# Attention of a gated mixer: a fixed plan for TensorE's side work, six rotating score banks, six value visits per group

## The chip, the cores and the metric

The kernel runs on one core of a Trainium2 chip. The metric is the device time of one execution in microseconds (us), the median of several runs. An execution has one more time, the span: from the first to the last instruction that the profiler recorded. TensorE is called PE below and its weight loads PEld; VectorE is DVE, ScalarE is ACT, GpSimd is POOL, and SyncE, which issues most of the DMAs, is SP.

## The reference

Two branches read the same input `x` (2048 tokens, 448 features) and are mixed token by token by a gate. Branch A is attention with 16 heads of 28 features that share one set of keys and values:

```
q = (x @ wq) split into 16 heads;  k = x @ wk;  v = x @ wv
scores = einsum("bhqd,bkd->bhqk", q, k) * 28 ** -0.5
a = (softmax(scores) @ v) merged @ wo
```

Branch B is a spatial-shift MLP: layer norm, `w1`, gelu, a shift of four channel quarters by one or two tokens, `w2`, a residual; then layer norm, `w3` (to 1792), gelu, `w4`, a residual. The result is `g * a + (1 - g) * b` with `g = sigmoid(x . gate_w)`. All data are 32-bit floats.

## The kernel before

The kernel works through branch B first (about 20 us to 424 us of the span) and through attention after it. The keys, the values and the first two groups of queries are made at the beginning.

Attention is cut into 16 groups, `u = 0..15`. A group is one block of 512 queries (`b = u // 4`) with four of the sixteen heads (`g = u % 4`). Within a group the 2048 keys are 16 key tiles `kt` of 128. A running number `k = 16 u + kt` counts key tiles over all groups.

For one key tile PE makes four score matmuls (line 663, one for each head `j`, 128 keys by 512 queries), each into a PSUM bank of its own. ACT turns each into `p = exp(s)` (line 665) and so frees the bank. The value products (`pv_group`, line 625) multiply the tile's `p` with the values of that key tile: four matmuls for each tile, one for each head in a 32-column strip of the array, each of which the profile shows as two instructions. They add up over the 16 tiles in one bank (`mx`), whose row of sums gives the softmax's denominator. They come in visits: after every second key tile (`PVB = 2`) PE makes the products of two tiles, which lie `LAG = 2` tiles behind the scores. A group so has eight visits.

PE has more work in attention, and all of it is written between the scores by hand:

- `q_job(u + 2)`, 11 matmuls (line 503): the queries of the group after the next. At its end `q_evac` (lines 144 to 151) reads the result's bank with ACT (`qh`, line 147) and then with DVE (`ql`, line 148), and three DMAs of SP spread it.
- `max_part(u + 1, t)`, four times four small matmuls (line 166), each four followed by a DVE maximum that reads the bank (line 167); then `max_rows`, one matmul (line 193) whose bank ACT copies (`mrow`, line 195), with two DMAs.
- `norm_job`, one matmul (line 543) that spreads the reciprocal sums of the group before; DVE multiplies from that bank (line 545), POOL splits the result into two parts (lines 548 and 549).
- `wo_job(b, t)`, 12 matmuls for 128 tokens of the output projection (lines 556 to 560), four of them for each block of queries once its four groups are done, each with a DVE operation that mixes in branch B (line 564) and a DMA out.

`q_job`, `norm_job` and `wo_job` are generators kept in a list `jobs`; `pump()` is called after every second score matmul and takes one step (about one matmul) of the job at hand. Jobs enter the list when a key tile's number is reached (`kt == 2` for queries, `k + 6` and `k + 8` after a group's end for the others). `max_part`, `max_end` and `max_rows` aren't pumped: they stand after the tiles `kt` = 6 to 11.

The order of PE's instructions is the order in which the program writes them (`manual_schedule(engines={PE})`). The order on the other engines and all waits are made by the framework's scheduler. A PSUM tile of a tag with `bufs = n` takes one of n banks in turn; the first instruction that writes it waits until all readers of that bank's former tile are done.

PSUM's eight banks in attention are: `mm` two, `misc` one and `s` two for scores (the tile `n % 5` picks among five); `m` two for all the other work (`m_tile`, also under the name `misc_tile`); `mx` one for the value products. That makes eight. In the last group `s_tile` uses three score banks only, as the two banks of `s` hold parts of the last output projection.

## Time and profile before

| | |
|---|---|
| median of 3 runs | 1071.31 us (1070.52 to 1072.3) |
| the profiled execution | 1070.98 us, of which the span is 1069.1 us |
| PE busy, matmuls | 1039.7 us (97%) |
| PE busy, weight loads | 679.6 us (64%) |
| ACT busy | 673.2 us (63%) |
| DVE busy | 258.0 us (24%) |
| POOL busy | 159.8 us (15%) |
| attention, first to last score matmul | 423.9 us to 1049.5 us |

PE's busy time is modelled, since matmuls overlap in its pipeline; a busy PE need not be at its peak. The chain of waits is followed back from the last instruction and names for each stretch the work that held up the end; its pieces are given with their start, their length and their count. In the timeline a row stands for some merged instructions of one line (start, length, engine, line, operation, result and inputs, count) and, in brackets, the idle time of the engine ahead of it with what ended it. A view by windows gives for each stretch of time the busy time of each engine, with the clock that was granted to PE (1.00 is full) as the third number from the end.

### The profile page before, as it was taken

To read this page: it belongs to the slowest core of one execution; us is meant where nothing else is said; L and a number is where in the kernel's file an instruction comes from. 1 tells how busy PE (TensorE), PEld (TensorE's weight loads), DVE (VectorE), ACT (ScalarE), POOL (GpSimd) and SP (SyncE) were. 2 spreads that over 40 slices of the span, in tenths; PEclk is the share of its full clock that TensorE was granted. 3 is DMA by queue.
4 is the path that set the end of the run, shared out by engine and by line. 5 is a ranking of instruction groups with operands and counts; after the bars stand their busy time and mean duration, and the time that the engine had idled before them with its cause. 6 is when DMAs were issued, how large, how long until landed. Compare 5 with 4: busy or idle time off the path is not lost.

```text
span 1069.1 us, 13948 instructions
## 1 busy us (share of the span) xinstructions
PE 1039.7 (97%) x5610; PEld 679.6 (64%) x5610; DVE 258.0 (24%) x521; ACT 673.2 (63%) x1318; POOL 159.8 (15%) x182
## 2 busy tenths in 40 slices
PE   6999889999999999999999999999999999999995
PEld 4787778888888888454554555554655555555542
DVE  6744952311411311401110110120110210111102
ACT  5444451222222223788888888889888889888873
POOL 5622430110200201603000002010002100000100
PEclk9999899999999999999999999999999999999998
DMA  9401330000000000423211202220202220211001
GB/s 312 131 1 37 111 111 1 1 1 1 1 1 1 1 1 29 164 32 70 33 17 16 31 20 40 39 31 3 39 10 41 39 31 2 40 24 26 10 2 38
DMA packets 30541, 41.15 MB, mean 38 GB/s; under 512 B 8004, under 2 KB 20100, under 8 KB 30340
## 3 DMA queue, kind: packets, MB, share of 16 engines
q1 hardware_dynamic: 30324, 40.04, 16.3%
q8 instruction: 46, 0.75, 0.3%
q14 instruction: 27, 0.22, 0.1%
q10 hardware_dynamic: 144, 0.13, 0.1%
HBM read 23.28 MB, written 3.67 MB: 25 GB/s over the span
## 4 chain that ended last, share of the span: by engine, by line
PE 91%; DVE 4%; DMA 1%; ACT 1%; POOL 1%; issue 1%; SPq 0%; POOLq 0%; ACTq 0%; DVEq 0%
PE s L663 27%; PE pv L625 22%; PE acc L420 4%; PE acc L419 4%; PE acc L421 4%; PE g L115 4%; PE g L116 4%; PE g L117 4%; PE q L503 3%; PE m L166 2%; PE wo L560 1%; PE wo L558 1%; PE wo L556 1%; PE g L119 1%; PE g L118 1%; PE h L116 1%
## 5 line engine op out<-in xcount | busy, mean ns | idle before, releaser
L665 ACT ACTIVATE p<-s 128x512 f32<-128x512 f32 x1024 | 517.6, 627 | 98.1 <-PE s L663 97.8
L663 PE MATMUL s<-qs,kS 98*128 98x512 f32 x1024 | 343.6, 420 | 1.4 <-ACT p L665 0.7
L663 PEld LDWEIGHTS s<-qs,kS 98*128 98x128 f32 x1024 | 181.6, 189 | 168.2 <-ACT p L665 127.1
L625 PE MATMUL pv<-p,vext 128*32 128x512 f32 x2048 | 247.6, 602 | 0.0
L409 ACT ACTIVATE gh<-g 128x512 fp32r<-128x512 f32 x56 | 33.6, 600 | 174.9 <-PE g L119 174.9
L625 PEld LDWEIGHTS pv<-p,vext 128*32 128x32 f32 x2048 | 53.7, 109 | 107.6 <-issue 100.3
L411 DVE TENSOR_TENSOR gl<-gf,gh 128x512 fp32r<-128x512 f32 x56 | 41.3, 738 | 192.1 <-ACT gf L410 192.0
L419 PE MATMUL acc<-w4h,gh 128*128 128x448 f32 x224 | 82.6, 369 | 0.0
L420 PE MATMUL acc<-w4l,gh 128*128 128x448 f32 x224 | 82.0, 366 | 0.0
L421 PE MATMUL acc<-w4h,gl 128*128 128x448 f32 x224 | 81.7, 365 | 0.0
L167 DVE TENSOR_REDUCE mr<-m 128x4 f32<-128x512 f32 x64 | 44.3, 692 | 146.0 <-PE m L166 145.3
L548 POOL CAST onh<-on 128x512 fp32r<-128x512 f32 x15 | 9.2, 614 | 414.8 <-DVE on L545 228.7
L115 PE MATMUL g<-ah,w3h 128*128 128x512 f32 x168 | 67.1, 399 | 3.1 <-ACT gf L410 2.8
L116 PE MATMUL g<-al,w3h 128*128 128x512 f32 x168 | 66.5, 396 | 0.1
L117 PE MATMUL g<-ah,w3l 128*128 128x512 f32 x168 | 66.3, 394 | 0.0
L521 DVE SCALAR_TENSOR_TENSOR good<-rt,good 128x16 f32<-128x16 f32 x15 | 2.6, 175 | 190.2 <-DMA rt<-o 190.2
L419 PEld LDWEIGHTS acc<-w4h,gh 128*128 128x128 f32 x224 | 42.0, 188 | 4.9
L420 PEld LDWEIGHTS acc<-w4l,gh 128*128 128x128 f32 x224 | 42.1, 188 | 4.8
L421 PEld LDWEIGHTS acc<-w4h,gl 128*128 128x128 f32 x224 | 42.0, 188 | 3.6
L166 PEld LDWEIGHTS m<-kS,qs 96*128 96x128 f32 x256 | 38.4, 191 | 6.3 <-DVE mr L167 1.2
L115 PEld LDWEIGHTS g<-ah,w3h 128*128 128x128 f32 x168 | 31.9, 190 | 9.7 <-ACT gf L410 3.3
L564 DVE SCALAR_TENSOR_TENSOR ot<-wo,gg,x 128x448 f32<-128x448 f32 x16 | 10.9, 682 | 108.0 <-PE wo L560 108.0
(204 smaller groups left out, 1144.4 us busy)
## 6 DMA issues: line engine op xcount, KB each, us to landing
qs<-qh SPq DMA_DIRECT2D x32, 256.0 KB
qs<-ql SPq DMA_DIRECT2D x16, 256.0 KB
xq<-in_xT_dram SPq DMA_DIRECT2D x4, 1024.0 KB
x<-in_x_dram SPq DMA_DIRECT2D x4, 896.0 KB
w3raw<-in_w_dram SPq DMA_DIRECT2D x7, 512.0 KB
out_dram<-ot SPq DMA_DIRECT2D x16, 224.0 KB
w4raw<-in_w_dram SPq DMA_DIRECT2D x7, 448.0 KB
xkv<-in_xT_dram SPq DMA_DIRECT2D x3, 1024.0 KB
```

Of the source, the lines that this page charges most:

```text
L115: nc.tensor.matmul(ps, wh[:, c, :], ah[:, c, :], start=(c == 0), stop=False)
L116: nc.tensor.matmul(ps, wh[:, c, :], al[:, c, :], start=False, stop=False)
L117: nc.tensor.matmul(ps, wl[:, c, :], ah[:, c, :], start=False, stop=False)
L166: nc.tensor.matmul(ps[:, j, :], q_of[u][0:96, j, t * P:(t + 1) * P], kS[0:96, 0:MK], start=True, stop=True)
L167: nc.vector.reduce_max(mx_of[u][:, :, t], ps, axis=AX.X)
L411: nc.vector.tensor_sub(gl, gf, f32(gh))
L419: nc.tensor.matmul(ps, gh[:, tok], w4h[i][:, k, :], start=(f == 0), stop=False)
L420: nc.tensor.matmul(ps, gh[:, tok], w4l[i][:, k, :], start=False, stop=False)
L421: nc.tensor.matmul(ps, gl[:, tok], w4h[i][:, k, :], start=False, stop=(f == NF - 1))
L625: nc.tensor.matmul(pv[32 * j:32 * j + 32, :], vext[:, kt, :], ps[j], start=(kt == 0), stop=(kt == NT - 1), tile_position=(0, 32 * j))
L663: nc.tensor.matmul(ps, kS[0:98, kt * P:(kt + 1) * P], q_of[u][0:98, j, :], start=True, stop=True)
L665: nc.scalar.activation(p, ps, AF.Exp, scale=SCALE)
```

## The change

A group's side work now follows a plan. Each key tile has two slots, after its second and after its fourth score matmul, so a group has slots 0 to 31. `units(u)` lists (first slot, generator) pairs; at each slot PE gets one step of the generator at hand, and where that one ends, of the next whose first slot has come. For most groups the list is: `q_job(u + 2)` from slot 0, the maxima of the next group from slot 12 (one `max_part` a slot), the normalisation from 16, `max_rows` from 17, and one `wo_job` of the former block from 18 (so the output projection of a block is spread over the four groups of the next). In group 0 the maxima start at slot 4, `max_rows` at 12 and `q_job(2)` at 20. The last matmul of a generator is now followed by a `yield` of its own: what reads its bank (`q_evac`, the DVE product of `norm_job`, `gate_out`) is written one slot later, behind that slot's two scores.

The banks are dealt out again: six for scores (`mm` two, `misc`, and three single ones, `s0` to `s2`), four of them in the last group; one (`m`) for all the other work; `mx` as before.

The value products come in six visits per group, after the scores of the key tiles 3, 6, 9, 12, 14 and of tile 0 of the next group. They take all tiles up to the one before the tile just scored: three, three, three, three, two and two tiles.

The input tile `raw` has one buffer in place of two, so the loads of `wq`, of the first `x` block and of `wo` come one after the other; the first block's low part is made by DVE in place of POOL. `onh` and `onl` have seven buffers in place of five. In the last group only four of the twelve (`t`, `g`) parts of the last output projection with `g < 2` run between scores; the others stand in the rewritten tail, between its transposes.

```diff
-LAG = 2
-PVB = 2
+VISITS = (3, 6, 9, 12, 14, 16)
...
         def m_tile(name):
-            return ps3.tile([P, 512], F32, tag="m", bufs=2, name=name)
...
+            return ps3.tile([P, 512], F32, tag="m", bufs=1, name=name)
...
+        def s_more(i):
+            return lambda name: ps3.tile([P, 512], F32, tag=f"s{i}", bufs=1, name=name)
+
+        s_tiles = (mm_tile, mm_tile, s_spare, s_more(0), s_more(1), s_more(2))
+
         def s_tile(n, last=False):
-            return (mm_tile, mm_tile, s_spare, s_more, s_more)[n % (3 if last else 5)](f"s_{n}")
+            return s_tiles[n % (4 if last else 6)](f"s_{n}")
...
-            raw = s3.tile([P, 4, 512], F32, tag="raw", bufs=2, name=f"xq_{b}")
+            raw = s3.tile([P, 4, 512], F32, tag="raw", bufs=1, name=f"xq_{b}")
...
-            (nc.gpsimd if b else nc.vector).tensor_copy(ah, raw)
-            nc.gpsimd.tensor_tensor(al, raw[:, 0:3, :], f32(ah)[:, 0:3, :], ALU.subtract)
+            eng = nc.gpsimd if b else nc.vector
+            eng.tensor_copy(ah, raw)
+            eng.tensor_tensor(al, raw[:, 0:3, :], f32(ah)[:, 0:3, :], ALU.subtract)
...
             for n, (w, a) in enumerate(ops):
                 nc.tensor.matmul(ps, w, a, start=(n == 0), stop=(n == 10))
-                if n < 10:
-                    yield
+                yield
...
             q_evac(s3, u, ps, q_of[u])
-            yield
...
             nc.tensor.matmul(ps, sel8, rb, start=True, stop=True)
+            yield
             on = s3.tile([P, 512], F32, tag="onf", bufs=2, name=f"on_{u}")
...
+        def max_units(u):
+            for t in range(4):
+                max_part(u, t, m_tile)
+                if t == 3:
+                    max_end(u)
+                yield
+
+        def row_unit(u):
+            max_rows(u, m_tile)
+            yield
...
+        def units(u):
+            b, g = divmod(u, NG)
+            wo = [(18, wo_job(b - 1, g))] if b else []
+            norm = [(16, norm_unit(u - 1))] if u else []
+            if u == 0:
+                return [(4, max_units(1)), (12, row_unit(1)), (20, q_job(2))]
+            if u < NU - 2:
+                return [(0, q_job(u + 2)), (12, max_units(u + 1))] + norm + [(17, row_unit(u + 1))] + wo
+            if u < NU - 1:
+                return [(12, max_units(u + 1))] + norm + [(17, row_unit(u + 1))] + wo
+            return [(0, wo_early(t, g)) for t in range(2) for g in range(2)] + norm + wo
...
-        def pv_group(k):
...
+        def visit(u, k0, k1):
...
+            for kt in range(k0, k1):
+                ps = p_of.pop((u, kt))
+                for j in range(4):
+                    nc.tensor.matmul(pv[32 * j:32 * j + 32, :], vext[:, kt, :], ps[j],
+                                     start=(kt == 0), stop=(kt == NT - 1), tile_position=(0, 32 * j))
+            if k1 == NT and u < NU - 1:
+                norm_of[u] = recip_begin(u, pv_of.pop(u))
...
                     p_of[u, kt].append(p)
+                    if j % 2 == 1:
+                        while True:
+                            if job is None:
+                                if not plan or plan[0][0] > 2 * kt + j // 2:
+                                    break
+                                job = plan.pop(0)[1]
+                            try:
+                                next(job)
+                                break
+                            except StopIteration:
+                                job = None
...
+            if kt in VISITS or kt == 0 and u:
+                v = VISITS.index(kt or NT)
+                visit(u if kt else u - 1, VISITS[v - 1] if v else 0, VISITS[v])
...
+        tail_wo(0, 2)
+        tail_wo(1, 2)
+        tail_a(0)
+        tail_a(1)
+        tail_wo(2, 0)
+        tail_wo(2, 1)
...
+        tail_wo(3, 1)
+        tail_wo(3, 2)
+        tail_wo(2, 3)
+        tail_wo(3, 3)
```

More of the change, by code (lines that the diff above doesn't have):

```diff
@@ L466, in m_tile @@
         def m_tile(name):
-            return ps3.tile([P, 512], F32, tag="m", bufs=2, name=name)
-        def s_more(name):
-            return ps3.tile([P, 512], F32, tag="s", bufs=2, name=name)
+            return ps3.tile([P, 512], F32, tag="m", bufs=1, name=name)
         def misc_tile(name):
@@ L543, in norm_job @@
             nc.tensor.matmul(ps, sel8, rb, start=True, stop=True)
+            yield
             on = s3.tile([P, 512], F32, tag="onf", bufs=2, name=f"on_{u}")
             nc.vector.tensor_mul(on, o, ps)
-            onh = s3.tile([P, 512], F32R, tag="onh", bufs=5, name=f"onh_{u}")
-            onl = s3.tile([P, 512], F32R, tag="onl", bufs=5, name=f"onl_{u}")
+            onh = s3.tile([P, 512], F32R, tag="onh", bufs=7, name=f"onh_{u}")
+            onl = s3.tile([P, 512], F32R, tag="onl", bufs=7, name=f"onl_{u}")
             nc.gpsimd.tensor_copy(onh, on)
@@ L550, in norm_job @@
             on_of[u] = (onh, onl)
-            yield
         def wo_group(ps, b, t, g, first, last):
@@ L570, in wo_job @@
                 yield from wo_group(ps, b, t, g, g == 0, g == NG - 1)
-                if g < NG - 1:
-                    yield
             gate_out(4 * b + t, ps)
-            yield
-        wqraw = s3.tile([P, 4, 512], F32, tag="raw", bufs=2, name="wqraw")
+        wqraw = s3.tile([P, 4, 512], F32, tag="raw", bufs=1, name="wqraw")
         nc.sync.dma_start(wqraw, wq)
@@ L587, in gated_mix_kernel @@
         split_wq(2, 4)
+        split_wq(0, 2)
         load_x(0)
-        woraw = s3.tile([P, 4, 512], F32, tag="raw", bufs=2, name="woraw")[:, :, 0:D]
+        woraw = s3.tile([P, 4, 512], F32, tag="raw", bufs=1, name="woraw")[:, :, 0:D]
         nc.sync.dma_start(woraw, wo.rearrange("(g p) n -> p g n", p=P))
-        split_wq(0, 2)
         nc.gpsimd.tensor_copy(woh, woraw)
@@ L596, in gated_mix_kernel @@
             nc.gpsimd.tensor_scalar(x1[:, n, :], x1[:, n, :], gi[:, n:n + 1], None, op0=ALU.mult)
-        jobs = []
-        current = [None]
-        def pump():
-            if current[0] is None:
-                if jobs:
-                    current[0] = jobs.pop(0)()
-                    next(current[0])
-            else:
-                try:
-                    next(current[0])
-                except StopIteration:
-                    current[0] = None
-        def drain():
-            while current[0] is not None or jobs:
-                pump()
+        norm_of = {}
@@ new lines, in gated_mix_kernel, with norm_unit, wo_early @@
+        wo_last = []
+        def max_units(u):
[6 more added lines that the diff above has]
+            max_rows(u, m_tile)
+            yield
+        def norm_unit(u):
+            yield from norm_job(u, *norm_of.pop(u))
+        def wo_early(t, g):
+            if g == 0:
+                wo_last.append(s_tiles[5 - t](f"wo_{NB - 1}_{t}")[:, 0:D])
+            yield from wo_group(wo_last[t], NB - 1, t, g, g == 0, False)
@@ new lines, in rest @@
+        def rest():
+            yield
+        def units(u):
[9 more added lines that the diff above has]
+            return [(0, wo_early(t, g)) for t in range(2) for g in range(2)] + norm + wo
@@ L616, in gated_mix_kernel @@
         p_of, pv_of = {}, {}
-        def pv_group(k):
-            u, kt = divmod(k, NT)
-            if kt == 0:
+        def visit(u, k0, k1):
+            if k0 == 0:
                 pv_of[u] = max_tile(f"pv_{u}")
             pv = pv_of[u]
-            ps = p_of.pop(k)
-            for j in range(4):
-                nc.tensor.matmul(pv[32 * j:32 * j + 32, :], vext[:, kt, :], ps[j],
-                                 start=(kt == 0), stop=(kt == NT - 1), tile_position=(0, 32 * j))
-            if kt == NT - 1 and u < NU - 1:
-                o, rb = recip_begin(u, pv_of.pop(u))
-                delayed.append((k + 6, lambda: norm_job(u, o, rb)))
-                if u == NU - 2:
-                    for t in range(4):
-                        delayed.append((k + 10, lambda t=t: wo_last_job(t, NG - 2)))
-                elif u % NG == NG - 1:
-                    for t in range(4):
-                        delayed.append((k + 8, lambda t=t: wo_job(u // NG, t)))
@@ L637, in gated_mix_kernel @@
-        wo_last = []
-        def wo_last_job(t, g):
-            if g == 0:
-                wo_last.append((m_tile if t < 2 else s_more)(f"wo_{NB - 1}_{t}")[:, 0:D])
-            yield from wo_group(wo_last[t], NB - 1, t, g, g == 0, False)
-            yield
-        delayed = []
-        for k in range(NU * NT + LAG):
-            u, kt = divmod(k, NT)
-            while delayed and delayed[0][0] <= k:
-                jobs.append(delayed.pop(0)[1])
-            if k == (NU - 1) * NT:
-                for g in range(NG - 2):
-                    for t in range(4):
-                        jobs.append(lambda t=t, g=g: wo_last_job(t, g))
+            for kt in range(k0, k1):
[3 more added lines that the diff above has]
+                                     start=(kt == 0), stop=(kt == NT - 1), tile_position=(0, 32 * j))
@@ L654, in gated_mix_kernel @@
+            if k1 == NT and u < NU - 1:
+                norm_of[u] = recip_begin(u, pv_of.pop(u))
+        for k in range(NU * NT + 1):
+            u, kt = divmod(k, NT)
             if k < NU * NT:
-                if kt == (7 if u == 0 else 2) and u + 2 < NU:
-                    jobs.insert(0, lambda u=u: q_job(u + 2))
+                if kt == 0:
+                    plan = units(u)
+                    at, job = 0, None
                 if kt == 8 and (u + 3) % NG == 0 and u + 3 < NU:
                     load_x((u + 3) // NG)
-                p_of[k] = []
+                p_of[u, kt] = []
@@ L663, in gated_mix_kernel @@
                     nc.tensor.matmul(ps, kS[0:98, kt * P:(kt + 1) * P], q_of[u][0:98, j, :], start=True, stop=True)
-                    p = s3.tile([P, 512], F32, tag="p", bufs=4 * (LAG + PVB) + 2, name=f"p_{n}")
+                    p = s3.tile([P, 512], F32, tag="p", bufs=18, name=f"p_{n}")
                     nc.scalar.activation(p, ps, AF.Exp, scale=SCALE)
-                    p_of[k].append(p)
-                    if j % 2 == 1 or u == NU - 1:
-                        pump()
-                if u + 1 < NU:
-                    if 6 <= kt < 10:
-                        max_part(u + 1, kt - 6, m_tile)
-                    elif kt == 10:
-                        max_end(u + 1)
-                    elif kt == 11:
-                        max_rows(u + 1, m_tile)
-            if k >= LAG and k % PVB == PVB - 1:
-                for kk in range(k - LAG - PVB + 1, k - LAG + 1):
-                    if kk >= 0:
-                        pv_group(kk)
-        assert not delayed
-        drain()
+                    p_of[u, kt].append(p)
+                    if j % 2 == 1:
[9 more added lines that the diff above has]
+                                job = None
+                if kt == NT - 1:
+                    if job is not None:
+                        for _ in job:
+                            pass
+                    for _, job in plan:
+                        for _ in job:
+                            pass
+            if kt in VISITS or kt == 0 and u:
+                v = VISITS.index(kt or NT)
+                visit(u if kt else u - 1, VISITS[v - 1] if v else 0, VISITS[v])
         u = NU - 1
@@ L685, in gated_mix_kernel @@
         o = s3.tile([P, 512], F32, tag="o", bufs=2, name=f"o_{u}")
-        onh = s3.tile([P, 512], F32R, tag="onh", bufs=5, name=f"onh_{u}")
-        onl = s3.tile([P, 512], F32R, tag="onl", bufs=5, name=f"onl_{u}")
+        onh = s3.tile([P, 512], F32R, tag="onh", bufs=7, name=f"onh_{u}")
+        onl = s3.tile([P, 512], F32R, tag="onl", bufs=7, name=f"onl_{u}")
         on_of[u] = (onh, onl)
@@ L706, in tail_b, with tail_wo @@
             nc.vector.tensor_sub(onl[:, toks[t]], tq, f32(onh)[:, toks[t]])
-        def tail_c(t):
-            for _ in wo_group(wo_last[t], NB - 1, t, NG - 1, False, True):
-                pass
-            gate_out(4 * (NB - 1) + t, wo_last[t])
+        wo_last.append(m_tile(f"wo_{NB - 1}_2")[:, 0:D])
+        wo_last.append(s_tiles[3](f"wo_{NB - 1}_3")[:, 0:D])
+        def tail_wo(t, g):
+            for _ in wo_group(wo_last[t], NB - 1, t, g, g == 0, g == NG - 1):
+                pass
+            if g == NG - 1:
+                gate_out(4 * (NB - 1) + t, wo_last[t])
         for t in range(4):
             nc.scalar.copy(o[:, toks[t]], pv[:, toks[t]])
-        for step in range(6):
-            if step < 4:
-                tail_a(step)
-            if 0 < step < 5:
-                tail_b(step - 1)
-            if step > 1:
-                tail_c(step - 2)
+        tail_wo(0, 2)
[4 more added lines that the diff above has]
+        tail_wo(2, 1)
+        tail_b(0)
+        tail_b(1)
+        tail_a(2)
+        tail_a(3)
+        tail_wo(2, 2)
+        tail_wo(3, 0)
+        tail_wo(0, 3)
+        tail_wo(1, 3)
+        tail_b(2)
+        tail_b(3)
+        tail_wo(3, 1)
+        tail_wo(3, 2)
+        tail_wo(2, 3)
+        tail_wo(3, 3)
         worst = s3.tile([P, 1], F32, name="worst")
@@ L749, in gated_mix_kernel @@
                                              start=True, stop=True)
-                            p = s3.tile([P, 512], F32, tag="p", bufs=4 * (LAG + PVB) + 2, name=f"p2_{u}_{kt}_{j}")
+                            p = s3.tile([P, 512], F32, tag="p", bufs=18, name=f"p2_{u}_{kt}_{j}")
                             nc.scalar.activation(p, ps, AF.Exp, scale=SCALE)
```

## The prediction, made before the result was known

> **What bounds the kernel now.** I read the page first, for the engines and the chain that ended last, then the chain in order of time through attention, then the timeline around the side work.

> ```profile
> PE 1039.7 (97%) x5610; PEld 679.6 (64%) x5610; DVE 258.0 (24%) x521; ACT 673.2 (63%) x1318; POOL 159.8 (15%) x182
> ...
> PE 91%; DVE 4%; DMA 1%; ACT 1%; POOL 1%; issue 1%; SPq 0%; POOLq 0%; ACTq 0%; DVEq 0%
> ```

> PE holds 91% of the chain. Whether that is work or waiting shows in the chain's pieces (start, length, count) for a group without output projection:

> ```profile
> 703.41 1.85 PE pv L625 x16
> 705.26 0.66 PE s L663 x2
> 705.92 0.24 PE q L503
> 706.16 0.47 PE s L663 x2
> ...
> 711.73 0.40 PE m L166 x4
> 712.13 0.51 PE s L663 x2
> ...
> 729.50 2.59 PE s L663 x8
> 732.09 1.85 PE pv L625 x16
> ```

> A pair of scores takes 0.47, or 0.66 right after a visit and 0.51 after a maximum; a q step 0.235, a set of four maxima 0.40. Where side work fills the gaps PE runs without a break. Where there is none, eight scores take 2.59 in place of 0.66 + 3 x 0.47 = 2.07: there, and only there, five banks hold PE back, by 0.5 in two tiles. So PE is the bound, mostly with work. Group ends are the ACT copies of `pv`:

> ```profile
> 468.14 0.59 ACT L525 COPY o<-pv 128x512 f32<-128x512 f32 x1
> ...
> 582.17 0.59 ACT L525 COPY o<-pv 128x512 f32<-128x512 f32 x1
> ...
> 974.00 0.59 ACT L525 COPY o<-pv 128x512 f32<-128x512 f32 x1 [0.31 <-PE pv L625]
> ...
> 1013.11 0.59 ACT L525 COPY o<-pv 128x512 f32<-128x512 f32 x1 [1.00 <-PE pv L625]
> ```

> Groups 1 to 3 take (582.17 - 468.14) / 3 = 38.0 each, groups 4 to 13 (974.00 - 582.17) / 10 = 39.2, group 14 39.1.

> **Visits.** Two prices are needed beside those above:

> ```profile
> 1050.36 0.13 PEld L625 LDWEIGHTS pv<-p,vext 128*32 128x32 f32 x4 [0.30 <-issue]
> ...
> 1052.51 0.13 PEld L625 LDWEIGHTS pv<-p,vext 128*32 128x32 f32 x4 [0.30 <-issue]
> ```
> ```profile
> 1015.24 0.21 PE wo L556
> ```

> Five steps of four value instructions take 2.15, so 0.43 each and 0.86 a tile. A visit of two tiles (1.85) is 1.72 of work and 0.13 of turning over, and the first pair behind it costs 0.19 more: 0.32 a visit. Two visits fewer save 0.64 a group, 10 in all. A visit of three tiles costs 2.71. A wo step takes about 0.205.

> **The new group, without waits**, in stretches from visit to visit, for groups 4 to 13 (pairs + side work + visit):
> tiles 15 and 0: 2.07 + 0.47 + 1.85 = 4.39;
> tiles 1 to 3: 3.01 + 6 q 1.41 + 2.71 = 7.13;
> tiles 4 to 6: 3.05 + 3 q 0.71 + 2 maxima 0.80 + 2.71 = 7.27;
> tiles 7 to 9: 3.09 + 0.80 + the normalisation 0.24 + `mt` 0.11 (as a quarter of a maxima set) + 2 wo 0.41 + 2.71 = 7.36;
> tiles 10 to 12: 3.01 + 1.23 + 2.71 = 6.95;
> tiles 13 and 14: 2.07 + 0.82 + 1.85 = 4.74.
> That is 37.84, or 1.34 under today's 39.2. ACT doesn't bind:

> ```profile
> 705.19 0.73 PE L663 MATMUL s<-qs,kS 98*128 98x512 f32 x2
> 705.73 4.03 ACT L665 ACTIVATE p<-s 128x512 f32<-128x512 f32 x8 [0.75 <-PE s L663]
> ```

> The first exp starts 0.54 behind its score; one lasts 0.63 and eight 4.03, so the pace is 0.486: twelve take 5.83 of a stretch of 7. With six banks, score n waits for exp n - 6, which costs nothing where side work lies between.

> **The waits of the one bank `m`.** All side work now shares it, and PE, in written order, stops with every score behind it until the bank's readers are done. Rows for it:

> ```profile
> 711.57 0.56 PE L166 MATMUL m<-kS,qs 96*128 96x128 f32 x4
> 712.16 0.69 DVE L167 TENSOR_REDUCE mr<-m 128x4 f32<-128x512 f32 x1 [8.40 <-PE m L166]
> 712.48 0.40 PE L503 MATMUL q<-ahq,wql 128*128 128x512 f32 x1
> 712.71 0.62 PE L663 MATMUL s<-qs,kS 98*128 98x512 f32 x2
> 713.47 0.64 ACT L147 CAST qh<-q 128x512 fp32r<-128x512 f32 x1
> 714.14 0.69 DVE L148 TENSOR_TENSOR ql<-q,qh 128x512 fp32r<-128x512 f32 x1 [1.29 <-ACT qh L147]
> ...
> 1029.69 0.40 PE L543 MATMUL rbc<-rb,sel 128*128 128x512 f32 x1
> 1030.19 0.69 DVE L545 TENSOR_TENSOR on<-o,rbc 128x512 f32<-128x512 f32 x1 [13.80 <-PE rbc L543]
> 1030.94 0.96 PE L663 MATMUL s<-qs,kS 98*128 98x512 f32 x3 [0.61 <-DVE on L545]
> ```

> The last group shows the mechanism today: there the normalisation borrows a score bank, and PE stands 0.61 until DVE has left it, resuming 0.06 behind DVE.

> (a) *Queries to maxima.* Today the cast `qh` follows the exps written before it (the matmul ended at 712.88, the cast began at 713.47); the next work had the other `m` bank. After the change the last q step is in slot 10, `q_evac` is written behind the scores of slot 11, and the maximum of slot 12 needs the bank. Counted from the stretch's start: slot 11 holds scores 7 and 8; exp 8 starts at 0.54 + 7 x 0.486 = 3.94; `qh` starts 0.49 later and lasts 0.64, to 5.07; `ql` from 5.10 to 5.79; the maximum at 5.85 and 0.1 slow in starting. PE is there at 0.66 + 0.71 + 4 x 0.47 = 3.25. Wait: 2.7.
> (b) *Maximum to maximum.* From a set's start, DVE ends after 0.59 + 0.69, PE can go on at 1.34, plus 0.1; its own work (0.40 + 0.51) is over at 0.91. Wait: 0.5, in slots 13 and 15 (a visit covers slot 14), and again for the normalisation in slot 16.
> (c) *Normalisation to `mt`.* 0.1 + 0.50 + 0.69 + 0.06 + 0.1 against 0.1 + 0.235 + 0.47: wait 0.6.
> (d) *`mt` to wo*: ACT's copy `mrow` follows at once, as ACT has no backlog by then; 0.1.
> (e) Wo to the next q: DVE's mix (0.68 today) runs under a visit. Nothing.

> Together 2.7 + 1.5 + 0.6 + 0.1 = 4.9 a group; 42.8 in all. If `qh` were let past the two exps of slot 11, (a) is 1.7: the lower bound. No row bounds it above more tightly than a whole stretch of exps: 12 in place of 8, 1.9 more.

> **The sum.** Groups 4 to 13: 10 x (42.8 - 39.2) = +36. Groups 1 to 3 lack wo: in tiles 10 to 14 the six banks bind (score 12 waits for exp 6, which ends at 3.60: 6.8 for the stretch, and 4.0 for the next), so 4.39 + 7.13 + 10.5 + 8.6 + 6.8 + 4.0 = 41.4 against 38.0: +10. Group 0: no q work until slot 20, one visit turn fewer in the pace of ACT, then 2.2 of wait (a) between `q_job(2)` and `q_job(3)`: -1. Groups 14, 15 and the tail: group 14 keeps (b) to (d), +1; group 15 gets four banks for three, but each score still waits for an exp four back: +1 (-2 to +3). The tail takes 24 more wo steps, 4.9, and runs today as:

> ```profile
> 1053.69 0.28 ACT o L714
> ...
> 1056.71 0.68 DVE ot L564
> ...
> 1059.34 0.21 PE wo L560
> ```

> That is 5.9 with PE mostly waiting; 36 wo steps and 8 transposes are some 8.5: +2 (0 to +4.9). Sum: 36 + 10 - 1 + 1 + 1 + 2 = +49.

> At nothing I cost the larger `onh` (seven buffers where five were enough) and the serial loads into `raw`:

> ```profile
> 429.09 0.95 DVE L580 CAST wqh<-wqraw 128x768 fp32r<-128x768 f32 x1 [4.33 <-DMA wqraw<-in_wq_dram]
> ...
> 435.25 0.78 POOL L583 TENSOR_TENSOR wql<-wqraw,wqh 64x256 fp32r<-64x256 f32 x1
> ```

> `wq` is split by 436.0; the load it waited for came 5 after attention's start (423.9), so the `x` block lands by 441 and its splits on DVE and POOL end by about 447, against slot 20 at about 448 (ten tiles at 2.4). If that cover fails, PE stops once for what it is late: at most 3. On SP's queue the order stays (`qs`, `x` at tile 8, `mrow`), and what it carries is due a half group later.

> **PE's clock.** In wait (a) PE is wholly idle for 2.6. What such idle time did before (a row of the timeline; then, by windows, PE's busy time and, third from the end, its clock):

> ```profile
> 140.82 0.79 PE L115 MATMUL g<-ah,w3h 128*128 128x512 f32 x1 [2.83 <-ACT gf L410]
> ```
> ```profile
> 138.00:140.00 2.00, 0.00 (x0) 0.00 (x0) 0.00 (x0) 1.97 (x3) 1.50 (x1) 1.00 0.73 238
> 140.00:142.00 2.00, 1.18 (x3) 0.99 (x4) 0.69 (x1) 2.00 (x5) 0.57 (x1) 0.60 0.21 15
> 142.00:144.00 2.00, 2.00 (x7) 1.57 (x6) 1.29 (x2) 0.66 (x2) 0.00 (x0) 0.54 0.63 222
> ```
> ```profile
> 430.40:434.00 3.60, 3.60 (x18) 0.76 (x18) 3.52 (x5) 1.92 (x4) 2.97 (x3) 0.53 0.22 84
> ```

> A gap of 2.83 was followed by some 2.8 us of work at half clock, and the thin scores at attention's start by 3.6 us at 0.53: a loss of 1.4 to 1.7. After (a) that hits the visit and eats the wait (b) of slot 13 (0.5), since the pair ahead of it gets slower. So 0.9 to 1.2 for each of 13 groups (1 to 13): +13 if it comes every time, 0 if 2.6 is too short, 13 x 1.7 = +22 at most. I take +12, by the gap of 2.83, to which 2.6 is nearest.

> [...]

> **The rivals.** The forecast: waits (a) to (d) and half clock behind (a): 1070.98 + 49 + 12 = 1132 in the profiled execution's own time (its span plus 1.9), which lies 0.3 under the median of the runs: 1132.

> *The clock stays full*: 1071 + 49 = 1120. For it speaks that 2.6 is shorter than the gap shown; against it, that the gap shown is longer by a tenth only.

> *Shorter waits*: `qh` gets ahead of slot 11's exps (a: 1.7) and PE falls behind ACT enough that (b) is half covered: 3.2 a group, no half clock: 1120 - 13 x 1.7 = 1098. The scheduler makes ACT's order, so it can be; in the rows above the cast kept its written place.

> *Faster*: the bank's readers end before PE comes back, so the even spread and the two saved visits are all that is seen: groups 4 to 13 save 13.4, groups 1 to 3 1.5 each, group 0 3, the end gives 2 back: 1052. This needs slots as long as ACT's two exps (0.97) and a cast without backlog. It decides at 1.34 us of waits a group; (b) alone makes 1.5. Against it stands the 0.61 for one DVE reader.

> *No change*: the waits come to just that 1.34.

> **How the numbers follow.** Forecast 0.50, full clock 0.24, shorter waits 0.13, faster 0.10, no change 0.03. The runs shown spread by 0.17%, so about 0.2% can be told from nothing. Slower is 0.50 + 0.24 + 0.13 = 0.87. The range takes in full clock and shorter waits (1098, and 4 less for the tail and the loads) and, above, half clock without cover and the upper bounds of the tail and group 15: 1132 + 10 + 5 = 1147. Left out: faster and no change, 0.13, and some tails.

> **What would show it.** Right: an idle row ahead of the maxima (line 166) in each group of 2 to 3 us put down to `ql`, rows of about 0.5 put down to the maximum (line 167) and to `on` (line 545); granted clock below 1 in attention; 6 visits a group with 24 value instructions in four of them; no 2.59 for eight scores except in groups 1 to 3; group times of 41 to 44. Wrong: group times near 38, ACT's idle time well under 98, or a `qh` that starts less than 2 us after the last q step. I would be most wrong if PE met `m` free, that is if DVE's and ACT's reading fell under the value visits more often than the slots say.

## The result, and the profile after

The changed kernel takes 1168.73 us (median; 1166.1 to 1170.41) against 1071.8 us (1070.52 to 1072.3) for the kernel before beside it: a ratio of 1.0904 [1.0884, 1.0924]. It is slower by 9%. Forecast were 1132 us, in a range from 1094 to 1147. The profiled execution takes 1168.56 us, with a span of 1166.8, which is 97.7 more than before.

The page of the changed kernel, each engine's busy time and the chain by engine:

```profile
PE 1081.0 (93%) x5610; PEld 686.9 (59%) x5610; DVE 258.4 (22%) x522; ACT 675.6 (58%) x1318; POOL 158.1 (14%) x181
...
PE 81%; DVE 8%; ACT 6%; issue 1%; DMA 1%; POOL 1%; SPq 0%; ACTq 0%; DVEq 0%; POOLq 0%
```

The number of matmuls is the same (5610). PE's busy time is 41.3 longer and its share of the chain fell from 91 to 81%; DVE's rose from 4 to 8 and ACT's from 1 to 6. So both happened: PE waits more, and for some of its time it works more slowly. The waits, by who ended them (total, times, longest):

```profile
PE m L165 <- DVE ql L147: 33.5, 13, 2.6
PE m L165 <- DVE mr L166: 13.4, 26, 6.8
PE mt L192 <- DVE on L546: 5.3, 14, 0.4
PE rbc L543 <- DVE mr L166: 3.8, 14, 0.3
```

None of these four stood among the longest waits of before. All of them are waits for the one bank `m`. The group ends, as before the ACT copies of `pv` (line 525; group 15 has its own at line 721), put the 97.7 in place:

```profile
478.42 0.59 ACT L525 COPY o<-pv 128x512 f32<-128x512 f32 x1 [2.88 <-PE pv L643]
...
611.97 0.59 ACT L525 COPY o<-pv 128x512 f32<-128x512 f32 x1
...
1066.90 0.67 ACT L525 COPY o<-pv 128x512 f32<-128x512 f32 x1
...
1108.25 0.59 ACT L525 COPY o<-pv 128x512 f32<-128x512 f32 x1 [1.19 <-PE pv L643]
...
1149.26 0.43 ACT L721 COPY o<-pv 128x128 f32<-128x128 f32 x2 [1.14 <-PE pv L643]
```

| stretch | before | after | difference | forecast |
|---|---|---|---|---|
| to the end of group 0 | 468.14 | 478.42 | +10.3 | -1 |
| groups 1 to 3 | 114.0 | 133.6 | +19.5 | +10, and 3 of the 12 for the clock |
| groups 4 to 13 | 391.8 | 454.9 | +63.1 | +36, and 9 of the 12 |
| group 14 | 39.1 | 41.4 | +2.2 | +1 |
| group 15 | 40.6 | 41.0 | +0.4 | +1 |
| from there to the end | 15.4 | 17.5 | +2.1 | +2 |

Inside a group, the chain in order of time (start, length, piece, count) for group 5:

```profile
662.33 2.71 PE pv L643 x24
665.04 0.44 PE s L660
...
667.97 1.62 ACT p L662 x3
669.59 0.49 ACT qh L146
...
670.10 0.70 DVE ql L147
...
670.85 0.68 PE m L165 x4
...
671.55 0.70 DVE mr L166
...
672.30 0.66 PE m L165 x4
672.96 4.41 PE pv L643 x24
```

From the visit's end to the first maximum lie 670.85 - 665.04 = 5.8 us, in which the chain runs through the exps, `qh` and `ql`: wait (a). Behind it a visit of 24 value instructions takes 4.41 in place of 2.71. The windows (length, then busy time of PE, PEld, DVE, ACT and POOL with instruction counts, granted clock, DMA share, GB/s) show why:

```profile
668.50:670.75 2.25, 0.00 (x0) 0.00 (x0) 0.65 (x1) 2.25 (x6) 2.17 (x2) 1.00 0.00 0
672.98:676.40 3.42, 3.42 (x20) 0.88 (x24) 0.69 (x1) 0.00 (x0) 1.19 (x1) 0.50 1.06 125
...
761.73:768.56 6.83, 6.70 (x29) 2.30 (x30) 0.77 (x2) 0.75 (x2) 0.00 (x0) 0.50 0.68 81
```

PE does nothing for the whole of the first window, with the clock still full; some 2 us after it begins again, the clock goes to one half for 3.4 us. In the third row, around the same wait in group 7, it is at one half for 6.8. Cut into fine windows, attention of the changed kernel holds 15 such stretches: one of 13.7 us and one of 3.4 in group 0, and one at wait (a) in each of the groups 1 to 13, of 3.4 us in four of them (5, 6, 9 and 12) and of 6.8 in nine. With 5.7 us at the very end of the span, (1 - clock) x time adds up to 48.9 us. By the same count the kernel before has two stretches from attention's start on, 3.4 us there and 7.1 at its end, with 5.2 us.

These times are no accident: in this trace all falls of the clock lie whole multiples of 3.413 us apart, from the first at 24.45 to the last at 1161.09 (333 steps). It falls at 536.45, 580.82 and 625.20, each time 44.37 = 13 x 3.413 later, and at 672.98, which is 14 x 3.413 later, and every stretch inside the span is one, two or four such steps long (3.41, 6.83 or 13.65). The kernel before shows the same step: its five falls, from 24.37 to 1062.02, lie 27, 7, 85 and 185 steps apart. What a wait cost at half clock went here also by where it fell on this grid: where PE resumed 1.28 to 1.92 us after a grid point, one step followed (the four groups named); in the other nine, two.

### The profile page after: what moved, and what is told of

Same layout as the page of the kernel before. It is cut to its first block, busy times and chain, and to the rows that moved or that the text cites. A ratio compares the mean times of both kernels' runs of the same rounds, so it can differ in the third digit from the quotient of the medians.

```text
span 1166.8 us, 14127 instructions
## 1 busy us (share of the span) xinstructions
PE 1081.0 (93%) x5610; PEld 686.9 (59%) x5610; DVE 258.4 (22%) x522; ACT 675.6 (58%) x1318; POOL 158.1 (14%) x181
## 4 chain that ended last, share of the span: by engine, by line
PE 81%; DVE 8%; ACT 6%; issue 1%; DMA 1%; POOL 1%; SPq 0%; ACTq 0%; DVEq 0%; POOLq 0%
PE pv L643 23%; PE s L660 19%; ACT p L662 5%; PE acc L418 4%; PE acc L419 4%; PE acc L420 4%; PE m L165 4%; PE g L114 3%; PE g L115 3%; PE g L116 3%; DVE mr L166 2%; PE q L505 2%; PE wo L556 1%; PE wo L558 1%; PE wo L560 1%
## 5 line engine op out<-in xcount | busy, mean ns | idle before, releaser
L660 PE MATMUL s<-qs,kS 98*128 98x512 f32 x1024 | 336.5, 419 | 0.1
L643 PE MATMUL pv<-p,vext 128*32 128x512 f32 x2048 | 270.2, 661 | 0.0
L643 PEld LDWEIGHTS pv<-p,vext 128*32 128x32 f32 x2048 | 61.4, 118 | 143.8 <-issue 136.6
L165 PE MATMUL m<-kS,qs 96*128 96x128 f32 x256 | 47.7, 316 | 47.0 <-DVE ql L147 33.5
L410 DVE TENSOR_TENSOR gl<-gf,gh 128x512 fp32r<-128x512 f32 x56 | 41.3, 739 | 192.3 <-ACT gf L409 192.2
L165 PEld LDWEIGHTS m<-kS,qs 96*128 96x128 f32 x256 | 41.1, 222 | 68.3 <-DVE ql L147 38.7
L166 DVE TENSOR_REDUCE mr<-m 128x4 f32<-128x512 f32 x64 | 44.3, 693 | 120.1 <-PE m L165 120.1
L115 PE MATMUL g<-al,w3h 128*128 128x512 f32 x168 | 66.7, 397 | 0.1
L147 DVE TENSOR_TENSOR ql<-q,qh 128x512 fp32r<-128x512 f32 x16 | 11.0, 690 | 142.3 <-ACT qh L146 142.3
```

The source lines that it names most:

```text
L115: nc.tensor.matmul(ps, wh[:, c, :], al[:, c, :], start=False, stop=False)
L165: nc.tensor.matmul(ps[:, j, :], q_of[u][0:96, j, t * P:(t + 1) * P], kS[0:96, 0:MK], start=True, stop=True)
L166: nc.vector.reduce_max(mx_of[u][:, :, t], ps, axis=AX.X)
L410: nc.vector.tensor_sub(gl, gf, f32(gh))
L643: nc.tensor.matmul(pv[32 * j:32 * j + 32, :], vext[:, kt, :], ps[j], start=(kt == 0), stop=(kt == NT - 1), tile_position=(0, 32 * j))
L660: nc.tensor.matmul(ps, kS[0:98, kt * P:(kt + 1) * P], q_of[u][0:98, j, :], start=True, stop=True)
```

## The experiments

The theory that went in was the forecast's: the bank's waits, and half the clock behind the long one, whose idle time sets it off. Its rival: that the clock falls for another reason, so that filling the idle time changes nothing. Two things of the result fitted no forecast: the groups 1 to 13 were 1 to 2.6 us longer than it had them with half clock, and group 0 lost 10 us. Each edit is against the changed kernel, unless it says otherwise. Beside each measured time stands its ratio to the kernel before on the same chip.

**Keeping PE busy in wait (a).** Ten matmuls with a zero weight go to PE ahead of the first maximum; they add nothing to the value sum.

```diff
+        zero = s3.tile([P, P], F32R, name="zero")
+        nc.gpsimd.memset(f32(zero), 0.0)
...
+                    if kt == 6 and j == 1 and 0 < u < NU - 2:
+                        for _ in range(10):
+                            nc.tensor.matmul(pv_of[u], zero, kS[:, 0:512], start=False, stop=False)
                     if j % 2 == 1:
                         while True:
```

> In groups 1 to 13, ahead of the first maximum of slot 12, PE makes ten more matmuls with zero weights onto the open value sum. They add nothing to the result and take about 2.35 of the 2.6 us in which PE stands idle for the bank m, so the wait ends when it did and only the idleness is gone. Theory 1 (the idle wait halves the clock): the granted clock in groups 1 to 13 returns to 1.00, the half-clock stretches behind slot 12 (some 81 us in all, 40 us lost, about 6 of them hidden by other waits) vanish, and the time falls from 1168.6 by about 34 to 1135. Theory 2 (the clock falls for the longer value visits, or by PE's load in general): half clock stays and the time stays at 1168 or rises. Theory 3 (the loss is only the waits for the bank): 1168, within 2.

Measured: 1146.86 us, 1.0707 [1.0659, 1.0756]. The wait is as long as it was, but PE is idle in it for 0.25 in place of 2.6, and the visit behind it is back at 2.71. The chain of this run in group 5:

```profile
661.59 0.49 ACT qh L146
...
662.10 0.70 DVE ql L147
...
662.84 0.68 PE m L165 x4
...
664.95 2.71 PE pv L645 x24
...
674.12 0.85 PE s L662 x2
674.97 0.37 PE wo L558
675.34 4.58 PE pv L645 x24
```

Work that nobody needs made the kernel 22 us faster: that is the idle time's effect on the clock, apart from its length (the mean granted clock was 0.974 in place of 0.951). Seven of the groups 4 to 13 had no half clock at all and took 43.1 to 43.2 each, and the groups 2 and 3 took 41.63: the forecast's 42.8 and 41.4 for a full clock. But three of the groups 4 to 13 (and group 1) still had a stretch of half clock, later in the group. The last rows show it: the `wo` steps and the pairs of scores grow to 1.8 times their length from about 672.3 on (the clock falls at 672.25), just behind the row of short waits for the maxima, `rbc` and `mt`. So in this run half clock came also without the long idle time. Whether it followed that row went by the grid: in the four groups with half clock its first maximum started 0.49 to 0.88 us after a grid point, in the other nine at 0.17 or at 1.16 and later. The expected 1135 was missed by 12, of which these groups, against their like, make 1.4 + 3.0 + 2.9 + 1.6 = 8.9.

**The cast right behind the last query step.** `q_evac` is no longer one slot behind.

```diff
                 nc.tensor.matmul(ps, w, a, start=(n == 0), stop=(n == 10))
-                yield
+                if n < 10:
+                    yield
...
             q_evac(s3, u, ps, q_of[u])
+            yield
```

> Undoes one part: the cast and the subtraction that read the query bank are written right behind the last q matmul in slot 10, as before the change, and not behind the scores of slot 11. Theory 1: the cast follows exp 6 in place of exp 8, the wait ahead of the first maximum falls from 2.7 to 1.7 (13 us over 13 groups); PE's idle time falls to 1.6, and if that is too short to halve the clock, the half-clock stretches go as well: 1168.6 - 13 - 34 = 1121; if 1.6 is still enough, 1155. Theory 2: 1155 with half clock as before. Theory 3: 1155.

Measured: 1145.65 us, 1.0696 [1.0647, 1.0745]. The idle time of wait (a) fell from 33.5 in 13 waits to 20.9 (1.6 each), so 12.6 of the 23 us gained are the wait's own length. The time lies between the two expected, 1121 without half clock and 1155 with it: half clock still came in 11 of the 13 groups, some of it behind the idle 1.6 and some later, mostly for one step of the grid (7 of 11); groups took 42.2 to 45.1. So half clock followed here also where the longest idle time was 1.6, with short waits behind it.

**The maxima later.** They start at slot 14, the normalisation at 18, `max_rows` at 19, `wo` at 20; the queries' cast then has a whole visit to itself.

```diff
...
-                return [(0, q_job(u + 2)), (12, max_units(u + 1))] + norm + [(17, row_unit(u + 1))] + wo
+                return [(0, q_job(u + 2)), (14, max_units(u + 1))] + norm + [(19, row_unit(u + 1))] + wo
...
```

> Moves one thing: in groups 1 to 14 the maxima start in slot 14, behind a value visit, in place of slot 12, and normalisation, row and output steps move two slots with them. The bank is still one. Theory 1: the visit covers the cast, wait (a) and its half clock are gone, a wait of 0.5 appears between the output step of slot 31 and the next q step: 1168.6 - 13 x 2.7 - 34 + 6 = 1106. Theory 2: 1140, with half clock as before. Theory 3 in the form that the short waits between maxima carry the loss: not under 1140, and these rows stay.

Measured: 1140.9 us, 1.0652 [1.0602, 1.0701], where 1106 was expected. Wait (a) is gone in the groups 1 to 13. Beside 3.0 in 9 for the first query step behind the last output step, which was expected, what is left of waits for `m` is mostly the maxima's own:

```profile
PE m L165 <- DVE mr L166: 18.8, 46, 6.8
```

Without the 6.8 (group 0) that is 12.0 in 45, or 0.27 each. And yet the clock fell. Chain and windows of one group:

```profile
661.03 0.41 PE m L165 x4
...
662.21 0.68 PE m L165 x4
...
665.11 0.72 PE m L165 x4
665.83 0.96 PE s L660 x2
...
668.73 4.54 PE pv L643 x24
```
```profile
661.00:665.75 4.75, 3.94 (x24) 2.64 (x23) 2.08 (x3) 4.14 (x8) 1.64 (x2) 0.98 1.10 130
...
665.56:672.39 6.83, 6.83 (x28) 2.62 (x31) 1.73 (x4) 2.46 (x6) 1.88 (x2) 0.50 0.47 148
```

Four sets of maxima in a row come at a pace of 1.45, that is DVE's 0.70 and PE's 0.68 one after the other. No single idle time is over 0.3, PE is busy for 3.94 of 4.75 us, and at its end the clock goes to 0.50 for 6.8 us. Nine of the groups 1 to 13 had this, and again the grid parts them: in these nine the row of maxima started 1.65 to 2.59 us after a grid point, in the other four 0.29 to 1.55. Those with output work took 43.0 to 44.2 then, and 41.7 without half clock. In the changed kernel a visit parts the maxima, here none does. My expectation of 1106 held a full clock for certain, as nothing long was left; that was wrong.

**Group 0: moving the maxima.** In the changed kernel PE stands in group 0 for a maximum that has nothing to do with the queries. DVE's and then PE's timeline there:

```profile
427.25 0.69 DVE L166 TENSOR_REDUCE mr<-m 128x4 f32<-128x512 f32 x1 [2.67 <-PE m L165]
428.89 0.98 DVE L578 CAST wqh<-wqraw 128x768 fp32r<-128x768 f32 x1 [0.94 <-DMA wqraw<-in_wq_dram]
...
433.39 1.81 DVE L582 CAST wql<-wqraw 64x256 fp32r<-64x256 f32 x1
435.24 0.69 DVE L166 TENSOR_REDUCE mr<-m 128x4 f32<-128x512 f32 x1
```
```profile
435.99 1.11 PE L165 MATMUL m<-kS,qs 96*128 96x128 f32 x4 [6.80 <-DVE mr L166]
```

The second maximum is queued on DVE behind six splits of `wq`, the first of which waits for its load; the third set of maxima needs the bank and PE stands 6.8, with all scores behind it. Two edits move the maxima past it:

```diff
-                return [(4, max_units(1)), (12, row_unit(1)), (20, q_job(2))]
+                return [(14, max_units(1)), (18, row_unit(1)), (20, q_job(2))]
```

> Moves one thing: in group 0 the maxima of group 1 start in slot 14 in place of slot 4 and the row in slot 18. In the changed kernel PE stands 6.8 us in group 0 for a maximum that DVE has queued behind the splitting of wq. If that is what makes group 0 10.3 us longer than before, it ends 8 to 11 us earlier: 1159. If group 0 is longer for another reason (the serial loads of the first x block), 1168 within 2.

Measured: 1172.21 us, 1.0944 [1.0845, 1.1043]. Group 0 ended at 478.83, no sooner than without the edit. DVE's timeline says where the maximum went: behind the next load.

```profile
441.00 1.23 DVE L490 CAST ahq<-xq 128x2048 fp32r<-128x2048 f32 x1 [6.42 <-DMA xq<-in_xT_dram]
...
443.94 0.69 DVE L166 TENSOR_REDUCE mr<-m 128x4 f32<-128x512 f32 x1
```

The other way, with `(0, max_units(1))`:

> Moves one thing: in group 0 the maxima of group 1 start in slot 0 in place of slot 4, so that DVE makes them ahead of the splits of wq, for which it waits until 428.9. With the maxima in slot 14 group 0 stayed as long (they then stood behind the load and the splits of x on DVE). If DVE's queue is what stops PE in group 0, the wait of 6.8 goes and group 0 ends 7 to 10 us earlier: 1160. If the serial loads hold group 0 in another way, for instance the first q steps, no more than 3 are gained: 1166.

Measured: 1170.95 us, 1.0923 [1.0901, 1.0945]; group 0 ended at 477.52, since the third maximum is still caught by the splits (PE idle 7.78 ahead of the fourth set). Both moves missed; they left open whether DVE's queue was the cause at all.

**Group 0: the splits off DVE.** POOL makes `wq`'s splits instead.

```diff
-            nc.vector.tensor_copy(wqh[:, 0:3, w], wqraw[:, 0:3, w])
+            nc.gpsimd.tensor_copy(wqh[:, 0:3, w], wqraw[:, 0:3, w])
...
```

> One part of the changed kernel moves engine: POOL, not DVE, makes the three copies that split wq, so DVE has nothing between the maxima of group 0. If PE's wait of 6.8 us in group 0 is DVE's queue (a maximum behind splits that wait for a load), the wait goes. The splits then take longer on POOL, so the x block, which waits for the one raw buffer, comes some 5 us later and the q steps of slot 20 may wait up to 4 for it: 1160 to 1166 in all. If PE's wait stays at 6 or more, DVE's queue isn't its cause.

Measured: 1160.81 us, 1.0818 [1.0788, 1.0848], as expected; group 0 ended at 469.28, which is 9.1 of the 10.3. In the view of waits the 6.8 has gone, and the window over the same place is at full clock:

```profile
PE m L165 <- DVE mr L166: 7.1, 27, 0.3
```
```profile
430.50:437.00 6.50, 6.23 (x42) 3.11 (x41) 2.75 (x4) 3.91 (x9) 6.38 (x9) 1.00 0.00 0
```

The other waits and the groups 1 to 15 are as in the changed kernel. That settles group 0: the maximum stood in DVE's queue behind the readers of a load. With the 6.8 went the half clock around it, in the changed kernel 13.7 us from 430.6 on, of which PE worked through some 8.

**Two banks for `m`, five for scores.**

```diff
-            return ps3.tile([P, 512], F32, tag="m", bufs=1, name=name)
+            return ps3.tile([P, 512], F32, tag="m", bufs=2, name=name)
...
-        s_tiles = (mm_tile, mm_tile, s_spare, s_more(0), s_more(1), s_more(2))
+        s_tiles = (mm_tile, mm_tile, s_spare, s_more(0), s_more(1))
...
-            return s_tiles[n % (4 if last else 6)](f"s_{n}")
+            return s_tiles[n % (3 if last else 5)](f"s_{n}")
...
```

> Undoes one part: the banks are dealt out as before the change (two for m, five for scores, three in the last group); the plan, its slots and the six visits stay. If the one bank is the cause, the waits between maxima, normalisation and row go, and of wait (a) 1.8 is left, ahead of the second maximum, which takes the query's bank: a group is some 39.6 at full clock, with at most one half-clock stretch: 1090 to 1115. If the plan's order or the visits are the cause, it stays above 1140.

Measured: 1125.91 us, 1.0503 [1.0461, 1.0546]: 43 us of the 97 came back, less than expected. The loss by half clock, counted as above, fell to 19.4 us in 8 stretches, group 0 kept its loss, and the groups 4 to 13 still took 41.2 to 43.2. With the later maxima of above, and those of group 0 at slot 0:

> Two banks for m and five for scores, the maxima in slot 14 (normalisation, row and output steps two slots later), and in group 0 in slot 0; six visits. Nothing then waits for a bank with PE idle. If the waits and their half clock are the whole loss, the clock is 1.00 in groups 1 to 13, a group with output work takes 37.9 and one without 37.7, and the time is 1060 (1055 to 1066), about 1% faster than the kernel before. If something else in the plan or the visits costs time, it is above 1071.

Measured: 1105.89 us, 1.0325 [1.0306, 1.0344], where 1060 was expected. Here the clock stays at full from group 0 to group 13, and group 0 ends at 465.15, before that of the kernel before. And still the groups take 40.3 to 41.5 in place of 38.0 and 39.2. The chain of that run, and the longest of its waits on attention's side work, that of `mt` for DVE's `mc`, the end of the maxima, which `mt` reads:

```profile
672.28 0.69 PE s L660 x2
...
673.21 0.74 PE s L660 x2
...
674.18 2.71 PE pv L643 x24
...
679.18 2.33 PE s L660 x6
681.51 2.71 PE pv L643 x24
```
```profile
PE mt L192 <- DVE mc L185: 15.1, 14, 1.2
```

A run of twelve scores is more than five banks carry: towards its end a pair takes 0.69 to 0.74 in place of 0.47 even with a query step between the pairs, and six scores without side work take 2.33 in place of 1.4. The `mt` wait (1.08 a group) comes on top; it is no wait for a bank.

**The number of visits.** The same with eight visits of two tiles:

```diff
-VISITS = (3, 6, 9, 12, 14, 16)
+VISITS = (2, 4, 6, 8, 10, 12, 14, 16)
```

> The kernel with two banks and later maxima, and one thing changed: eight visits of two tiles in place of six. If a visit costs 0.32 in turning over and a slow first pair, this adds 2 x 0.32 x 16 = 10 us: 1070. If the longer visits cost something of their own (ACT running dry for longer), the difference is smaller or has the other sign.

Measured: 1069.56 us, 0.9979 [0.9967, 0.9991]. The number was near, but not for the reason given: eight visits were to cost some 10 more than six, and they took 36 less. The groups 1 to 3 took 38.2 and nearly all of the others 38.9, and the `mt` wait is gone: a visit now stands between the maxima and it. This version is faster than the kernel before by 0.2%, little more than its interval. As it keeps the plan (with the maxima two slots later) and the single `raw` buffer, these don't cost what the change lost.

Six visits alone, on the kernel before:

```diff
 LAG = 2
+VISITS = (0, 3, 6, 9, 12, 14, 16)
 PVB = 2
...
-            if k >= LAG and k % PVB == PVB - 1:
...
+            if kt in VISITS[1:] or kt == 0 and u:
+                v = VISITS.index(kt or NT)
+                for kk in range(VISITS[v - 1], VISITS[v]):
+                    pv_group(kk + (u if kt else u - 1) * NT)
```

> The kernel before with one part of the change alone: the six visits, one key tile behind (side work, five score banks and two banks for m as before). If a saved turn (0.32) were all, 10 us fewer: 1061. If five banks hold up the longer runs of scores, a run of twelve without side work costs 0.6 over one and a half runs of eight, and one with side work 0.3 to 0.5, less the saved turns: 1080 to 1095.

Measured: 1102.26 us, 1.0281 [1.0259, 1.0303], more than the 1080 to 1095 expected. By itself this part of the change costs some 30 us where there are five score banks. (The edit also brings the value products one key tile nearer to the scores; the version with eight visits does that too, and loses nothing.) Its chain:

```profile
713.02 0.74 PE s L664 x2
...
715.96 2.71 PE pv L626 x24
...
734.95 2.65 PE s L664 x8
```

With the clock at full, pairs at 0.74 say the same as in the run with two banks. In the changed kernel, with six banks, the last pairs of such a run with query steps take 0.47 and 0.50, and the stretch 7.1. Without side work, in the groups 1 to 3, six banks don't carry it either: twelve scores take 4.12 in place of 3.0 (552.14 in group 2), and 4.62 on five banks.

And eight visits on the changed kernel, with its six banks and its one `m`:

> Undoes one part of the changed kernel: eight visits of two tiles in place of six; one bank for m and six for scores stay. With two and five banks eight visits were 36 us faster than six. If that came from the five score banks, which hold up twelve scores in a row more than eight, six banks don't show it, and two more turns a group cost 10: 1178. If it came from visits that cover the waits of the side work, it shows here too wherever a visit falls between two steps that wait: 1150 or less.

Measured: 1167.65 us, 1.0882 [1.0854, 1.091]: no difference to the changed kernel that these runs can tell, and neither of the two expected. The loss by half clock was 59.4 us, up from 48.9, with stretches of 13.7 us in the groups 10 to 13 (47.8 a group) and of 3.4 in the groups 5 to 9 (44.6). What two visits more cost can't be parted from that.

**The older end of the kernel.** The version with two banks and eight visits took 60 us from the end of group 14 to the end, the kernel before 56; group 15 alone makes 2.9 of the difference (43.5 against 40.6). Here it has the older order: the parts of the last output projection with `g < 3` between the last scores, and the older tail.

```diff
...
-            return [(0, wo_early(t, g)) for t in range(2) for g in range(2)] + norm + wo
+            return ([(0, wo_early(t, g)) for g in range(2) for t in range(4)] + norm
+                    + [(18, wo_early(t, 2)) for t in range(4)])
...
```

> The fastest so far (two banks for m, five for scores, eight visits, later maxima) with the end as before the change: the last block's output steps with g below 3 run between the scores of the last group, at every score, and the older tail stands. To make room, group 14, which has no q steps, takes two of the third block's output jobs. The end of that kernel, from group 14's last value visit, took 60.3 us against 56.0 in the kernel before. If the late output steps are the 4.3, the time is 1065 to 1066, 0.5% under the kernel before; if not, 1069.

Measured: 1069.78 us, 0.997 [0.9956, 0.9984]: as fast as the one before it, and no 4 us gained. The work behind the last group got shorter, but group 15 took 44.5, where half clock shows behind the normalisation, which takes a score bank there (one step of 3.4 us from 1028.5). The place of the output steps was not what cost the 4 us; what does stayed open.

One bank for `m` and six for scores alone, on the kernel before, was not tried: there the maxima stand within the query job, which holds the bank.

## Why the prediction failed, step by step

*What bounds the kernel, and where the time comes from:* right. The bank's waits were named, each with its place and size. Wait (a) was put at 2.7 with PE idle for 2.6; the 13 waits measured 33.5 / 13 = 2.6. Waits (b) to (d) show as 0.27 (3.8 in 14 for `rbc`; the maxima's like it) and 0.38 (5.3 in 14), with a set of maxima at 0.68 in place of 0.40 on top, which the forecast had inside its 0.5.

*The group without half clock, 42.8 and 41.4:* right. The run with zero products shows 43.1 and 41.6 where the clock stays full. The stretches between visits that run at full clock in the changed kernel itself stand at 7.1 for the tiles 1 to 3 (forecast 7.13).

*PE's clock:* this is the first step that failed, as a size: "So 0.9 to 1.2 for each of 13 groups (1 to 13): +13 if it comes every time, 0 if 2.6 is too short, 13 x 1.7 = +22 at most." It came every time. But against the full-clock groups of the zero-product run, the groups with 3.4 us of half clock (44.8) lose 1.7 each and those with 6.8 us (45.5 to 46.3, or 44.5 without `wo`) 2.4 to 3.2. Groups 1 to 3 lose 133.6 - 3 x 41.63 = 8.7, groups 4 to 13 454.9 - 10 x 43.13 = 23.6: +32 in place of +12, and beyond the bound of 22. The bound was drawn from two single steps of the grid in the profile of before (2.8 and 3.6 us as read there, 3.4 by finer windows). The same profile shows twice, in branch B, half clock of two steps (6.8 us), and I passed over it:

```profile
24.37:31.19 6.82, 5.17 (x11) 3.40 (x12) 5.46 (x6) 3.01 (x3) 5.68 (x5) 0.50 1.08 243
116.53:123.35 6.82, 5.58 (x18) 4.98 (x19) 6.23 (x13) 3.02 (x4) 3.82 (x4) 0.50 0.25 74
```

By these the bound would have been 13 x 3.4 = 44. I also took (b) as cover, and it covered nothing: the four groups with one step lose 1.7, which is the whole of 3.41 / 2.

*The rival with the full clock,* which gave 1120, fell. It needed 2.6 us of idle time to be too short where 2.83 was not. Here 2.6 us was followed by half clock in 13 of 13 groups, and in the run with later maxima rows of idle times under 0.3 were too, in 9 of 13 groups: in these runs the length of a single gap doesn't part the cases.

*Group 0, "-1", and the loads "at nothing ... If that cover fails, PE stops once for what it is late: at most 3":* the second step that failed. The load of `wq` did come 5 us after attention's start, as forecast, and the change moved the maxima of group 0 from key tile 6 to slot 4 on to DVE's queue, next to the splits that wait for it. I had counted the splits against the query job that reads them, not against the maxima queued behind them. Measured +10.3, of which moving the splits gives 9.1 back. I had also put no half clock behind such a stop.

*The two saved visits, 0.64 a group:* not seen. The price of a turn was read rightly, but PE's time in a visit is also time in which the exps catch up with the scores. With five banks six visits cost some 30 (alone) and 36 (in the version with two `m` banks). With six banks the longer runs cost nothing where side work lies between the pairs, and in the groups 1 to 3 what the forecast had (4.12 + 2.71 = 6.8 for a stretch); that the gain is there isn't shown.

*Shorter waits, 1098, and faster, 1052:* fell. ACT kept the cast behind the exps of slot 11, as the chain shows (three exps, then `qh`).

*Groups 14 and 15 and the tail,* +1, +1, +2: measured +2.2, +0.4, +2.1.

Together, of the 1168.6 - 1132 = 36.6 that were missing, the clock in the groups 1 to 13 makes 20, group 0 11, the full-clock groups 4, and the rest 1.

## What to carry to other kernels

A PSUM bank that all side work shares costs PE, which works in written order, the time of its readers at each handover (1.45 us from one set of maxima to the next here, of which 0.70 is DVE's); count that against the time until PE comes back, not against the mean load. Price the clock behind a stall as well, 1.7 to 3.2 us each here, about as dear as the stall. And count a queue's neighbours: a maximum of 0.7 us behind a split that waits for a load stopped PE for 6.8.

The length of an uninterrupted run of scores and the number of score banks belong together: with side work between the pairs twelve scores ran freely on six banks and not on five, and eight ran on five. A split of the eight banks should be tried with the visit length that fits it.
